# The next pair of heads' bias read in nine pieces over three units, and the first two units without transfers of their tails, in a transformer block on one core

## The chip, the core and the metric

The kernel runs on one core of a Trainium2 chip. The metric is device time in microseconds (us) of one execution. Engines are named as in the profile: PE (TensorE's matmuls), PEld (its weight loads), DVE (VectorE), ACT (ScalarE), POOL (GpSimd) and SP (SyncE), which here does nothing but issue transfers; with "q" behind the name the engine's sequencer is meant.

## The reference, cut to what matters

Three stages follow each other: attention over 4 batches and 8 heads with a position bias, and two feed-forward stages. The change touches attention alone.

```python
B, H, S, D = q.shape                            # 4, 8, 576, 64
scores = (1 / np.sqrt(D)) * q @ k.transpose(0, 1, 3, 2)
x = (log1p(abs(pos_i - pos_j)) / log1p(max(pos_i, 1)))[..., None]
bias = maximum(x @ w1 + b1, 0) @ w2             # 576 x 576 for each of 8 heads
attn = exp(scores + bias - rowmax)
out = (attn / attn.sum(-1)) @ v
x = out as (batch, 576, 512)
x = x + relu(norm(x) @ w_ch1) @ w_ch2
x = x + (gated unit of x) @ w_out
```

## The kernel before, in words

**Stages.** A first stage (0 to about 53 us) computes the bias of all heads and stores it in DRAM (`scr`, `store`, line 358). Attention follows (53 to about 346 us), then the two feed-forward stages (to the end), which the change leaves alone.

**Units.** Attention has 16 units: a pair of heads `hp` (0 to 3) and a batch `b`, with `u = 4 hp + b`. A unit has nine tiles of scores, of 128 rows by 576: four for each head (tiles 0 to 3 and 5 to 8), and tile 4 with the last 64 rows of both. Each tile goes through `S` (scores on PE, line 693), `add` (DVE adds the bias and takes the minimum of the negated sum, line 708), `exp` (ACT, line 723), `T` (PE transposes 512 of the 576 columns, line 728), `hi` (ACT copies the rounded upper part, line 790) and `lo` (DVE subtracts it from the value, line 794). The product with V then takes upper and lower parts as separate terms (`PV`, line 801): for each head h and each half x of the 576 rows there are nine matmuls, of which the ninth multiplies the tails. `Pev`, `O`, `Oev`, `Or`, `fo`, `oc`, `ra`, `rb`, `fx`, `xr` bring the result back into rows, divide it and store it in DRAM (`xs`).

**Tails.** The last 64 of the 576 columns of each tile are transposed apart (`RT`, line 737). The matmul wants their upper parts on one half of the partitions and their lower parts on the other, in the tile `RT`. `RThi` (ACT) writes the upper parts; `RTlo` (DVE, line 763) writes the lower parts to a tile `TL` on the partitions where they arise; `RTd` (line 767) moves them across the partitions by transfers on SP's queue, two for each head (`RTd 0`, `RTd 1`, line 770) and one for tile 4 (`RTd 2`, line 772). The ninth matmul of a head waits for these to land. `RTx` (line 774) is the other way, until now used once at the end: DVE writes the lower parts straight to the other half of the partitions, in two subtractions of 64 partitions in place of one of 128.

**The order of work** is written out by hand: `FIRST` for unit 0, `SEQ` for each of units 1 to 15, `END` for the rest. An entry such as `0 T 3` is a step of the present unit, `-1` of the one before, `1` of the next; each engine runs its own share of the list in that order. `slot` steps (line 894) start transfers: `slot 0` the placing of the next unit's Q (four transfers), `slot 1` the last stores of the unit before, `slot 5` the loads of q and k two units ahead. `vh` (POOL) splits the next v and then issues the load of v two units ahead, `fx` (POOL) divides the result and issues its store. `C` and `cp` are pieces of a conversion of weights that runs beside (DVE, and POOL at `cp`).

**SP's queue.** All of these transfers are issued by SP in the list's order, and each waits for what it needs before the next can be issued.

**Bias.** A pair's bias (nine tiles of 128 x 576) lies in one of two buffers. Before the change `load_bias` (line 265) reads the next pair's whole bias in the unit with b = 2, in eight transfers at slots 1, 4 and 7. The tiles in `TURNED` are stored with their last 64 columns in front, and take two transfers (`turned`, line 260). The first pair's bias is read in the first stage at the places in `READ` (lines 80 and 370), between the last stores of `scr` (`finish`, line 380); two of the last stores are issued by ACT (line 367), the others by SP. Three large stores of `scr` that the first pair doesn't need are held back to unit 0 and the start of unit 1 (`HELD`, line 404).

**Later loads.** In units 12 and 13, weights for the next stage (line 605) are loaded in four transfers; the rows of `xs` (line 627) are loaded behind `fx`, four transfers for each of two batches (line 849).

Of the kernel before, what the change touches and what calls it, by code (L numbers as in the profile page):

```python
# [39 lines left out]
    S 0, S 1, slot 0, slot 1, add 0, add 1, C 0, exp 0, S 2, add 2, T 0, S 5, S 3, hi 0, C 1, add 5, exp 1, lo 0, exp 2, S 6, slot 2, T 1, T 2, add 3,  # L40
    add 6, exp 3, RT 3 0, hi 2, hi 1, lo 2, RT 1 0, S 4, S 7, slot 3, exp 5, lo 1, kh, add 7, T 3, RThi 0, T 5, hi 5, exp 6, hi 3, exp 7, +S 0, RTlo 0,
    lo 5, lo 3, slot 4, slot 5, T 6, RT 6 1, add 4, S 8, RTd 0, exp 4, RT 4 0, vh, RThi 2, T 4, +add 0, +S 2, RTlo 2, hi 4, cp, add 8, lo 4, slot 6,
    hi 6, RTd 2, sq, exp 8, PV 0 0 0 4, slot 7, +S 1, PV 0 0 4 8, lo 6, RT 8 1, T 7, RThi 1, +add 1, +add 2, PV 0 0 8 9, T 8, +S 3, Pev 0 0, RTlo 1,
    hi 7, PV 0 1 0 8, slot 8, lo 7, +exp 0, PV 0 1 8 9, +S 4, +exp 1, hi 8, RTd 1, Pev 0 1
""".split(",")]

LN_AT = [(), (), ((0, 0), (0, 1)), ((0, 2), (0, 3)), ()]
# [3 lines left out]
    O 0 2, RTx 1, lo 8, O 0 3, F 3, PV 1 0 0 5, O 0 0, PV 1 0 5 8, PV 1 0 8 9, Pev 1 0, ra, O 0 1, PV 1 1 0 1, N 0, N 1, Oev 0, fo 0, PV 1 1 1 8,  # L51
    PV 1 1 8 9, O 1 0, Pev 1 1, O 1 2, oc, O 1 1, O 1 3, Or, Oev 1, H 0 0 6, rb, R 0, fo 1, R 1, xr, fx, P 0, H 0 6 12, P 1, P 2, P 3, H 1 0 12
# [27 lines left out]
READ = {20: [2], 27: [0], 29: [1], 32: [3], 35: [4]}  # L80
# [20 lines left out]
def block_kernel(  # L101
# [175 lines left out]

    with ExitStack() as c:
# [306 lines left out]
    def open_first():  # L588
# [11 lines left out]
        for z in range(4):  # L600
# [15 lines left out]
            when(12, 1, ld)  # L616
            when(12, 5 + z, f0)
# [41 lines left out]
    with ExitStack() as c:  # L659
# [176 lines left out]
        def emit_fx(u):  # L836
# [12 lines left out]
            if ("loads", u) in M:  # L849
                M["loads", u]()  # L850
# [38 lines left out]

        def emit_C(u, j):  # L890
# [3 lines left out]
        def emit_slot(u, n):  # L894
# [41 lines left out]
        for u in range(1, NU):  # L936
            for w in SEQ:
# [4 lines left out]
                if 0 <= v < NU:  # L942
# [513 lines left out]
```

## Time and profile before

| what | time |
|---|---|
| three runs | 971.35, 973.46 (median), 974.78 us |
| the profiled execution, its own time | 970.38 us |
| its span, first to last instruction | 968.5 us |
| PE busy over the span | 923.5 us (95%) |
| DVE, ACT, POOL busy | 717.1, 497.5, 416.2 us |
| mean granted clock of TensorE | 0.987 |

The profiled execution is 3.1 us below the median of the runs. In the rows, `out<-in` names what an instruction writes and reads, `x` is a count, and what stands behind `<-` in a list of waits is what ended the wait. A granted clock of 1.00 stands for 2.4 GHz, of 0.50 for 1.2 GHz. Matmuls are pipelined, so that a busy PE isn't PE at its peak.

### The profile page before, as it was taken

To read this page: it belongs to the slowest core of one execution; us is meant where nothing else is said; L and a number is where in the kernel's file an instruction comes from. 1 tells how busy PE (TensorE), PEld (TensorE's weight loads), DVE (VectorE), ACT (ScalarE), POOL (GpSimd) and SP (SyncE) were. 2 spreads that over 40 slices of the span, in tenths; PEclk is the share of its full clock that TensorE was granted. 3 is DMA by queue.
4 is the path that set the end of the run, shared out by engine and by line. 5 is a ranking of instruction groups with operands and counts; after the bars stand their busy time and mean duration, and the time that the engine had idled before them with its cause. 6 is when DMAs were issued, how large, how long until landed. Compare 5 with 4: busy or idle time off the path is not lost.

```text
span 968.5 us, 16023 instructions
## 1 busy us (share of the span) xinstructions
PE 923.5 (95%) x5617; PEld 806.2 (83%) x5617; DVE 717.1 (74%) x1386; ACT 497.5 (51%) x1092; POOL 416.2 (43%) x547
## 2 busy tenths in 40 slices
PE   7878899799899999999999999999999999999998
PEld 2268899799799988888888888888888998988996
DVE  7976799699677978777769897989946556455452
ACT  8967799699788965322223132323222635344340
POOL 0056669668698754321314343333400522234151
PEclk9999899899999999999999999999999999999999
DMA  6877856856866173212022323323230200101001
GB/s 229 268 245 218 240 169 171 248 171 167 251 189 170 40 250 114 66 32 96 23 93 88 120 88 110 100 88 109 92 112 24 116 1 1 44 1 55 1 34 65
DMA packets 65247, 113.77 MB, mean 117 GB/s; under 512 B 13328, under 2 KB 28304, under 8 KB 64912
## 3 DMA queue, kind: packets, MB, share of 16 engines
q1 hardware_dynamic: 64768, 112.18, 37.2%
q8 instruction: 44, 0.72, 0.3%
q10 hardware_dynamic: 400, 0.58, 0.2%
q14 instruction: 35, 0.29, 0.1%
HBM read 70.33 MB, written 28.38 MB: 102 GB/s over the span
## 4 chain that ended last, share of the span: by engine, by line
PE 82%; DMA 7%; DVE 6%; issue 2%; ACT 2%; SPq 0%; POOL 0%; DVEq 0%; ACTq 0%; POOLq 0%
PE psh L124 20%; PE psy L124 20%; PE psa L124 10%; PE psa L1300 6%; PE s L706 6%; PE PB L811 5%; PE psa L1282 5%; PE pt L732 4%; DMA rt<-tl 4%; DVE m L335 2%; DVE ct L712 2%; PE pt L487 1%; DMA scr<-o 1%; PE OB L817 1%; DVE at0l L120 1%
## 5 line engine op out<-in xcount | busy, mean ns | idle before, releaser
L124 PE MATMUL psh<-blk,w1h 128*128 128x512 f32 (+1 forms) x640 | 151.2, 368 | 0.0
L655 ACT ACTIVATE hh<-psh 128x512 fp32r<-128x512 f32 (+1 forms) x80 | 44.1, 553 | 199.2 <-PE psh L124 199.1
L176 POOL TENSOR_TENSOR cvl<-cvl,cvt 128x512 f32<-128x512 f32 x44 | 56.9, 1292 | 205.8 <-DVE cvt L173 182.1
L124 PEld LDWEIGHTS psh<-blk,w1h 128*128 128x128 f32 x640 | 113.4, 189 | 20.5
L712 DVE CUSTOM_DVE_ANT_0 ct<-s,bias 128x576 f32<-128x576 f32 x144 | 106.6, 748 | 16.8 <-ACT rt L117 7.1
L726 ACT ACTIVATE a<-ct,sm 128x576 f32<-128x576 f32 x144 | 111.6, 777 | 4.9 <-DVE sm L712 4.8
L1103 DVE TENSOR_TENSOR x_sb<-psy,x_sb 128x512 f32<-128x512 f32 x144 | 97.3, 683 | 9.1 <-PE psy L124 8.6
L656 DVE SCALAR_TENSOR_TENSOR hl<-psh,hh 128x512 fp32r<-128x512 f32 (+1 forms) x80 | 50.5, 632 | 57.8 <-ACT hh L655 57.8
L124 PE MATMUL psy<-w2h,hh 128*128 128x512 f32 x288 | 90.1, 394 | 0.0
L732 PE MATMUL pt<-ident,a 128*128 128x128 f32 x576 | 87.7, 281 | 1.7 <-DVE at1l L120 1.6
L124 PE MATMUL psy<-w2l,hh 128*128 128x512 f32 x288 | 88.9, 390 | 0.0
L124 PE MATMUL psy<-w2h,hl 128*128 128x512 f32 x288 | 88.7, 389 | 0.0
L124 PE MATMUL psh<-blk,w1l 128*128 128x512 f32 (+1 forms) x320 | 78.7, 368 | 0.0
L706 PE MATMUL s<-kh,q 128*128 128x288 f32 x320 | 74.0, 321 | 1.9 <-DVE sm L712 1.2
L732 PEld LDWEIGHTS pt<-ident,a 128*128 128x128 f32 x576 | 71.3, 145 | 3.8 <-ACT at0h L117 1.5
L706 PE MATMUL s<-kl,q 128*128 128x288 f32 x320 | 67.2, 300 | 0.0
L124 PEld LDWEIGHTS psh<-blk,w1l 128*128 128x128 f32 x320 | 56.9, 189 | 10.0
L124 PEld LDWEIGHTS psy<-w2l,hh 128*128 128x128 f32 x288 | 54.0, 188 | 11.5
L124 PEld LDWEIGHTS psy<-w2h,hl 128*128 128x128 f32 x288 | 54.0, 188 | 11.5
L177 POOL TENSOR_TENSOR cvw<-cvl,cvw 128x512 f32<-128x512 f32 x44 | 59.9, 1362 | 3.4
L124 PEld LDWEIGHTS psy<-w2h,hh 128*128 128x128 f32 x288 | 52.6, 188 | 9.6
L120 DVE TENSOR_TENSOR at1l<-pt,at1h 128x512 fp32r<-128x512 f32 (+1 forms) x80 | 50.3, 630 | 12.6 <-ACT at1h L117 12.6
(185 smaller groups left out, 2136.5 us busy)
## 6 DMA issues: line engine op xcount, KB each, us to landing
r<-in_moe_w_ch_dram SPq DMA_DIRECT2D x32, 512.0 KB, 4.5
k<-in_k_dram SPq DMA_DIRECT2D x16, 640.0 KB, 6.1
q<-q SPq DMA_DIRECT2D x64, 144.0 KB, 2.5
scr<-o SPq DMA_DIRECT2D x24, 295.5 KB, 3.3
v<-in_v_dram SPq DMA_DIRECT2D x16, 320.0 KB, 3.3
q<-in_q_dram SPq DMA_DIRECT2D x16, 288.0 KB, 4.4
bias<-scr SPq DMA_DIRECT2D x8, 576.0 KB, 5.7
bias<-scr SPq DMA_DIRECT2D x8, 512.0 KB, 5.0
```

Of the source, the lines that this page charges most:

```text
L120: (eng or dve).tensor_tensor(out=o, in0=i, in1=hi.bitcast(F32), op=ALU.subtract)
L124: pe.matmul(ps, lhsT=w, rhs=x, start=start and j == 0, stop=stop and j == len(terms) - 1)
L176: pool.tensor_tensor(out=T["l"], in0=T["l"], in1=T["t"].bitcast(F32), op=ALU.mult)
L177: pool.tensor_tensor(out=T["w"], in0=T["l"], in1=T["w"], op=ALU.add)
L656: dve.scalar_tensor_tensor(out=hl[:, f, :n], in0=ps[:, :n], scalar=0.0, in1=hh[:, f, :n].bitcast(F32), op0=ALU.max, op1=ALU.subtract)
L706: pe.matmul(s[:, x, :288], lhsT=w, rhs=m[:, 288 * x:288 * x + 288], start=j == 0, stop=j == len(prs) - 1)
L712: dve.tensor_tensor_reduce(out=ct, in0=s[:, :, :288], in1=bias[UNITS[u][0]][:, n].rearrange("p (a b) -> p a b", a=2), scale=-0.125, scalar ...
L726: act.activation(weights(n), ct.rearrange("p a b -> p (a b)"), AF.Exp, scale=-1.0, bias=mt, accum_out=SU[u % 2][:, n:n + 1])
L732: pe.transpose(PA[k % 2][:, j], e[:, 128 * j:128 * j + 128], ident)
L811: pe.matmul(d, lhsT=w, rhs=m, start=q == 0, stop=q == len(terms) - 1)
L1103: dve.tensor_tensor(out=x_sb[:, t], in0=ps, in1=x_sb[:, t], op=ALU.add)
L1300: pe.matmul(ps[:, z, :288], lhsT=v, rhs=w[:, 288 * z:288 * z + 288], start=(q == 0), stop=(q == len(terms) - 1))
```

## The change

Each pair's next bias is read tile by tile (fourteen transfers in place of eight), at two new steps `B 0` and `B 1` in the units with b = 1, 2 and 3. In units 0 and 1, `RTx` takes the place of `RTlo` and `RTd`; for tile 4 it is one subtraction. The loads of weights in units 12 and 13 are split into two and two; the loads of `xs` rows go from `fx` to `slot 8`, behind the tails' transfers. The last two bias stores are issued by SP in place of ACT, and tiles 3 and 8 of the first pair's bias are read after all stores have been issued. The three lists have new orders: in `SEQ`, `slot 5` now stands behind `RTd 2` and `RTd 0`, `slot 0` and `slot 1` stand earlier. The changed list `FIRST` (with `RTx` for `RTlo` and `RTd`) and the changed list `END` hold otherwise the same steps as before, and are left out below.

```diff
@@ -25,31 +25,32 @@
 TURNED = (0, 2, 5, 7)
 
 SEQ = [w.strip() for w in """
-    -1 ra, 0 add 3, 0 T 0, -1 lo 8, 0 exp 2, 0 exp 3, -1 O 0 1, -1 O 0 0, 0 hi 0, -1 PV 1 0 0 5, 0 add 4, 0 slot 0, 0 slot 1, 0 RT 1 0, 0 T 1, 0 C 0,
-    0 lo 0, 0 RT 3 0, 0 C 1, -1 PV 1 0 5 8, 0 exp 4, -1 O 0 2, 0 hi 1, -1 O 0 3, -1 PV 1 0 8 9, -1 Pev 1 0, 0 S 5, 0 lo 1, 0 S 6, 0 RThi 0, 0 add 5,
-    0 T 2, -1 Oev 0, 0 RTlo 0, 0 hi 2, 0 RT 4 0, 0 slot 2, -1 PV 1 1 0 1, -1 PV 1 1 1 8, 0 slot 3, 0 kh, -1 PV 1 1 8 9, 0 add 6, 0 exp 5, 0 T 3,
-    -1 Pev 1 1, 0 RThi 2, 0 slot 4, 0 S 7, 0 lo 2, -1 rb, 0 hi 3, 0 RTlo 2, -1 O 1 2, -1 O 1 3, -1 O 1 1, 0 exp 6, 0 T 4, 0 slot 5, 0 add 7, 0 lo 3,
-    0 S 8, -1 O 1 0, 1 S 0, -1 fo 0, 0 hi 4, 0 RT 6 1, 0 PV 0 0 0 2, 0 RTd 2, 0 add 8, 0 T 5, 0 exp 7, 0 lo 4, 0 RTd 0, 0 vh, 1 add 0, -1 oc,
-    0 PV 0 0 2 8, -1 Oev 1, 0 T 6, 0 cp, 0 hi 5, -1 fo 1, 1 S 2, 0 PV 0 0 8 9, -1 fx, 0 sq, 0 slot 6, 0 exp 8, 0 lo 5, 0 slot 7, -1 Or, 0 RT 8 1, 0 hi 6,
-    0 lo 6, 0 Pev 0 0, 0 RThi 1, 1 exp 0, 1 S 1, 0 T 7, -1 xr, 0 RTlo 1, 0 T 8, 1 add 1, 0 RTd 1, 0 PV 0 1 0 8, 1 add 2, 0 PV 0 1 8 9, 0 hi 7, 0 slot 8,
-    0 hi 8, 0 lo 7, 1 S 3, 1 exp 1, 1 S 4, 0 Pev 0 1
+    0 T 0, 0 exp 2, 0 slot 0, 0 add 3, 0 exp 3, 0 slot 1, -1 PV 1 0 0 5, 0 C 0, 0 RT 1 0, -1 lo 8, 0 hi 0, 0 S 5, 0 RT 3 0, -1 PV 1 0 5 8, -1 O 0 2,
+    0 add 4, -1 O 0 3, 0 C 1, 0 RThi 0, 0 lo 0, -1 O 0 1, -1 PV 1 0 8 9, 0 T 1, 0 add 5, 0 S 6, 0 B 0, -1 O 0 0, 0 exp 4, -1 Pev 1 0, 0 RTlo 0, 0 RT 4 0,
+    0 hi 1, 0 slot 2, 0 exp 5, -1 ra, 0 slot 3, 0 T 2, 0 lo 1, 0 hi 2, -1 Oev 0, -1 PV 1 1 0 1, 0 add 6, -1 PV 1 1 1 8, -1 PV 1 1 8 9, 0 T 3, 0 lo 2,
+    0 S 7, -1 O 1 0, 0 RThi 2, -1 O 1 2, 0 kh, 0 RTlo 2, -1 Pev 1 1, 0 hi 3, -1 rb, 0 T 4, 0 exp 6, -1 fo 0, -1 oc, 0 hi 4, 0 add 7, 0 lo 3, 0 S 8,
+    -1 O 1 1, 0 RTd 2, 0 slot 4, -1 O 1 3, 0 RTd 0, 0 add 8, 1 S 0, 0 lo 4, -1 Oev 1, 0 slot 5, 0 PV 0 0 0 2, 0 T 5, 0 PV 0 0 2 8, 1 add 0, 0 T 6,
+    0 exp 7, 1 S 2, 0 hi 5, 0 RT 6 1, 0 exp 8, 0 RT 8 1, 0 vh, 0 cp, 0 lo 5, 0 hi 6, 1 S 1, 0 PV 0 0 8 9, -1 fo 1, -1 Or, 0 lo 6, 0 RThi 1, 0 Pev 0 0,
+    -1 fx, 0 RTlo 1, 0 T 7, 0 RTd 1, 0 T 8, 1 add 1, 1 add 2, 0 PV 0 1 0 8, 0 B 1, 0 PV 0 1 8 9, 0 sq, 0 slot 6, 1 exp 0, 0 hi 8, 0 slot 7, 1 S 3,
+    0 hi 7, -1 xr, 1 exp 1, 0 slot 8, 0 lo 7, 0 Pev 0 1, 1 S 4
 """.split(",")]
 
...
+B_AT = [(0,), (1, 2), (3,), (4, 5), (6,), (7, 8)]
...
@@ -77,7 +78,7 @@
     AA AA AA AA AA AA AA AA AD DD AA DA
 """.split()
 
-READ = {20: [2], 27: [0], 29: [1], 32: [3], 35: [4]}
+READ = {20: [2], 27: [0], 29: [1], 35: [3, 8, 4]}
 
 FULL = 24
 GROUPS = ((3, 2), (1, 3))
@@ -262,21 +263,20 @@
         sp.dma_start(out=dst[..., 64:], in_=src[..., :512])
         sp.dma_start(out=dst[..., :64], in_=src[..., 512:])
 
-    def load_bias(hp, z):
+    def load_bias(hp, n):
 
         if hp not in bias:
             new_bias(hp)
-        if z < 2:
-            t = bias[hp][:, 5 * z:5 * z + 4]
-            src = rows(2 * hp, 0, 512)[:, z].rearrange("(n p) j -> p n j", p=128)
-            turned(t[:, ::2], src[:, ::2])
-            sp.dma_start(out=t[:, 1::2], in_=src[:, 1::2])
+        t = bias[hp]
+        if n == 4:
+            for h in range(2):
+                sp.dma_start(out=t[64 * h:64 * h + 64, 4], in_=rows(2 * hp, 512, 64)[:, h])
+            return
+        src = rows(2 * hp, 128 * (n % 5), 128)[:, n // 5]
+        if n in TURNED:
+            turned(t[:, n], src)
         else:
-            for h in range(2):
-                sp.dma_start(out=bias[hp][64 * h:64 * h + 64, 4], in_=rows(2 * hp, 512, 64)[:, h])
-
-
-
+            sp.dma_start(out=t[:, n], in_=src)
 
     with ExitStack() as c:
         p = new_pool("bk", 1, c)
@@ -364,12 +364,11 @@
                 f += heads * PITCH
                 dims, src = [[H * PITCH, 16]], src[heads::H]
             dims += [[16 * (H * PITCH - 1), n], [1, 591]]
-            q = act if heads == 1 and z + n > 34 else sp
-            q.dma_start(out=bass.AP(scr.tensor, scr.offset + f, dims), in_=src.rearrange("p (s j) -> p s j", s=n))
+            sp.dma_start(out=bass.AP(scr.tensor, scr.offset + f, dims), in_=src.rearrange("p (s j) -> p s j", s=n))
 
         def read(k):
-            if k == 4:
-                load_bias(0, 2)
+            if k in (3, 4, 8):
+                load_bias(0, k)
                 return
             t, src = bias[0][:, k::5], rows(0, 128 * k, 128)
             if k % 2:
@@ -613,8 +612,8 @@
                 for k in range(2 if z < 2 else 0):
                     pool.tensor_scalar(out=T["t"][:, k], in0=T["t"][:, k], scalar1=gains[:, 2 * z + k:2 * z + k + 1], scalar2=0.0, op0=ALU.mult, op1=ALU.add)
 
-            when(12, 1, ld)
-            when(12, 5 + z, f0)
+            when(*((12, 1), (12, 1), (12, 8), (12, 8))[z], ld)
+            when(*((12, 5), (12, 6), (13, 1), (13, 2))[z], f0)
             when(13, 4 + z, lambda T=T: pool_copy(T["o"][0], T["t"]))
             when(*LO_AT[z], lambda T=T: split_lo(T["o"][1], T["t"], T["o"][0], pool))
         xT[0] = block_pair(M["wa0"])
@@ -773,6 +772,9 @@
 
         def emit_RTx(u, h):
             p, _ = tails(u, h)
+            if h == 2:
+                split_lo(tail(2, 1, 0), p, tail(2, 1, 1))
+                return
             for x in (1, 0):
                 split_lo(tail(h, x, 1 - x), p[half(x)], tail(h, x, x))
 
@@ -846,8 +848,6 @@
                 M["last x"] = store
             else:
                 store()
-            if ("loads", u) in M:
-                M["loads", u]()
 
         def emit_Or(u):
             pe.transpose(PB[:, 288:416], Pr.rearrange("p h c -> p (h c)"), ident)
@@ -886,6 +886,12 @@
                 split_v(u + 1)
             if u < NU - 2:
                 load_v(u + 2)
+
+        def emit_B(u, j):
+            hp, b = UNITS[u]
+            if hp < 3 and b:
+                for n in B_AT[2 * b - 2 + j]:
+                    load_bias(hp + 1, n)
 
         def emit_C(u, j):
             for f in conv_at.pop((u, j), []):
@@ -911,11 +917,11 @@
                 conv_first(new_pool("arc", 2, M["rc"]))
             if u == 12 and n == 0:
                 open_first()
-            if hp < 3 and b == 2 and n in (1, 4, 7):
-                load_bias(hp + 1, n // 3)
+            if n == 8 and ("loads", u - 1) in M:
+                M["loads", u - 1]()
 
         emit = dict(
-            slot=emit_slot, sq=emit_sq, kh=emit_kh, vh=emit_vh, C=emit_C, cp=lambda u: emit_C(u, 2), S=emit_S, add=emit_add, exp=emit_exp, T=emit_T, hi=emit_hi, lo=emit_lo, RT=emit_RT, RThi=emit_RThi,
+            slot=emit_slot, B=emit_B, sq=emit_sq, kh=emit_kh, vh=emit_vh, C=emit_C, cp=lambda u: emit_C(u, 2), S=emit_S, add=emit_add, exp=emit_exp, T=emit_T, hi=emit_hi, lo=emit_lo, RT=emit_RT, RThi=emit_RThi,
             RTlo=emit_RTlo, RTd=emit_RTd, RTx=emit_RTx, PV=emit_PV, Pev=emit_Pev, O=emit_O, Oev=emit_Oev, fo=emit_fo, fx=emit_fx, Or=emit_Or, oc=emit_oc, ra=emit_ra, rb=emit_rb, xr=emit_xr,
         )
         def first_T(j):
@@ -939,7 +945,9 @@
                 v, args = u + int(du), list(map(int, args))
                 if v == NU - 1 and name in ("RTlo", "RTd") and args == [1]:
                     continue
-                if 0 <= v < NU:
+                if v == 1:
+                    name = {"RTlo": "RTx", "RTd": ""}.get(name, name)
+                if 0 <= v < NU and name:
                     emit[name](v, *args)
                 elif v == NU and name in ("S", "add") and args[0] < 4 - (name == "add"):
                     (first_T if name == "S" else first_split)(*args)
```

## Rows read from the trace of the kernel before

**Rows 1.** The page, part 1: busy time, share of the span, count.

```profile
PE 923.5 (95%) x5617; PEld 806.2 (83%) x5617; DVE 717.1 (74%) x1386; ACT 497.5 (51%) x1092; POOL 416.2 (43%) x547
```

**Rows 2.** PE's waits, 45 to 350 us: total, times, longest.

```profile
PE PB L811 <- DMA rt<-tl: 24.1, 6, 6.0
PE pt L732 <- DVE at1l L120: 1.6, 2, 1.3
```

**Rows 3.** Windows by unit: length; PE, PEld, DVE, ACT, POOL busy; clock; DMA; GB/s.

```profile
53.34:68.97 15.63, 11.18 (x73) 9.53 (x72) 10.35 (x25) 9.83 (x24) 10.53 (x10) 0.94 0.76 239
68.97:91.61 22.64, 17.84 (x126) 17.62 (x125) 13.48 (x35) 15.38 (x40) 10.08 (x11) 0.89 0.80 241
91.61:107.45 15.84, 15.84 (x130) 15.68 (x129) 15.16 (x37) 15.54 (x42) 12.39 (x15) 1.00 0.76 218
107.45:129.59 22.14, 17.76 (x127) 17.51 (x126) 14.20 (x37) 15.52 (x39) 12.31 (x15) 0.85 0.69 212
...
176.76:200.88 24.12, 18.09 (x127) 17.81 (x126) 14.24 (x36) 15.89 (x40) 13.55 (x16) 0.86 0.66 201
...
247.96:269.69 21.73, 17.18 (x127) 16.94 (x125) 14.22 (x37) 15.53 (x39) 13.24 (x16) 0.92 0.65 200
...
285.21:303.17 17.96, 15.75 (x128) 15.55 (x127) 13.38 (x35) 15.10 (x40) 14.69 (x20) 1.00 0.60 169
303.17:321.10 17.93, 15.78 (x128) 15.55 (x127) 13.29 (x35) 15.10 (x40) 14.01 (x18) 1.00 0.50 144
321.10:336.75 15.65, 15.34 (x124) 14.94 (x123) 15.35 (x41) 14.96 (x40) 12.85 (x28) 1.00 0.14 35
```

**Rows 4.** SP's timeline in unit 6: start, time to issue, line, transfer.

```profile
169.36 0.58 SPq L262 DMA_DIRECT2D bias<-scr  x1
...
173.67 0.42 SPq L216 DMA_DIRECT2D k<-in_k_dram  x1
...
175.28 2.17 SPq L770 DMA_DIRECT2D rt<-tl  x2
```

**Rows 5.** The chain of waits, 170 to 190 us: start, length, what.

```profile
175.28 9.01 DMA rt<-tl
```

**Rows 6.** SP's timeline at the end of unit 4, without bias.

```profile
148.67 0.38 SPq L843 DMA_DIRECT2D xs<-x  x1
149.14 1.11 SPq L770 DMA_DIRECT2D rt<-tl  x2
```

**Rows 7.** The tails' transfers (line 770), from issue to landing.

```profile
DMA to landing us min/median/max: 1.9/2.0/9.1
```

**Rows 8.** PE's timeline, the matmul that waits for the transfers of rows 6.

```profile
153.79 0.38 PE L811 MATMUL PB<-rt,v 128*128 128x288 f32 x1
```

**Rows 9.** SP's timeline, the later loads in units 12 and 14.

```profile
278.81 2.00 SPq L605 DMA_DIRECT2D t<-wc  x4
...
308.07 1.75 SPq L627 DMA_DIRECT2D t<-xs  x4
```

**Rows 10.** Window 67 to 83 us, with the columns of rows 3.

```profile
67.00:83.00 16.00, 11.21 (x63) 10.92 (x64) 7.62 (x18) 8.07 (x21) 6.79 (x7) 0.79 0.99 287
```

**Rows 11.** SP's timeline in unit 0, the held stores of the bias.

```profile
62.51 1.21 SPq L368 DMA_DIRECT2D scr<-o  x2
```

**Rows 12.** DVE's groups by form to 350 us: busy us, mean ns, idle before.

```profile
L120 DVE TENSOR_TENSOR tl<-s,rt 128x256 fp32r<-128x256 f32 x31 | 13.0, 420 | 3.6 <-PE s L706 1.6 <-ACT rt L117 0.5 <-DMA bias<-scr 0.2
L120 DVE TENSOR_TENSOR rt<-s,rt 64x256 fp32r<-64x256 f32 x2 | 0.8, 422 | 0.1
```

**Rows 13.** SP's waits, 45 to 350 us.

```profile
SPq L843 <- POOL x L840: 23.1, 13, 4.2
```

**Rows 14.** DMA issues: what, count, KB each, median us to landing.

```profile
bias<-scr SPq DMA_DIRECT2D x8, 512.0 KB, 5.0
bias<-scr SPq DMA_DIRECT2D x8, 64.0 KB, 4.6
```

**Rows 15.** The page, part 5: the group of `exp` on ACT.

```profile
L726 ACT ACTIVATE a<-ct,sm 128x576 f32<-128x576 f32 x144 | 111.6, 777 | 4.9 <-DVE sm L712 4.8
```

More of the change, by code (lines that the diff above doesn't have):

```diff
@@ L39 @@
 FIRST = [w.strip() for w in """
[L40 to L44, printed above, removed]
+    S 0, add 0, exp 0, S 1, S 2, add 1, exp 1, add 2, S 5, T 0, hi 0, S 3, exp 2, T 1, add 5, RT 1 0, slot 0, lo 0, exp 5, S 6, T 2, hi 2, add 3, hi 1,
+    add 6, S 4, slot 1, lo 2, C 0, exp 3, lo 1, S 7, T 3, T 5, C 1, add 4, slot 2, add 7, exp 6, slot 3, hi 3, hi 5, S 8, kh, slot 4, RT 3 0, lo 3,
+    exp 4, add 8, slot 5, +S 0, RThi 0, vh, T 4, lo 5, +S 1, T 6, exp 8, +add 0, RT 4 0, hi 4, RTx 0, PV 0 0 0 4, RThi 2, RTx 2, lo 4, exp 7, hi 6, +S 2,
+    lo 6, RT 8 1, cp, slot 6, RT 6 1, PV 0 0 4 8, RThi 1, +add 1, PV 0 0 8 9, sq, T 8, Pev 0 0, T 7, PV 0 1 0 8, +S 3, +add 2, RTx 1, +exp 0, hi 7,
+    PV 0 1 8 9, hi 8, slot 7, +S 4, lo 7, +exp 1, slot 8, Pev 0 1
 """.split(",")]
+B_AT = [(0,), (1, 2), (3,), (4, 5), (6,), (7, 8)]
 LN_AT = [(), (), ((0, 0), (0, 1)), ((0, 2), (0, 3)), ()]
@@ L50 @@
 END = [w.strip() for w in """
-    O 0 2, RTx 1, lo 8, O 0 3, F 3, PV 1 0 0 5, O 0 0, PV 1 0 5 8, PV 1 0 8 9, Pev 1 0, ra, O 0 1, PV 1 1 0 1, N 0, N 1, Oev 0, fo 0, PV 1 1 1 8,
-    PV 1 1 8 9, O 1 0, Pev 1 1, O 1 2, oc, O 1 1, O 1 3, Or, Oev 1, H 0 0 6, rb, R 0, fo 1, R 1, xr, fx, P 0, H 0 6 12, P 1, P 2, P 3, H 1 0 12
+    RTx 1, O 0 0, PV 1 0 0 5, lo 8, F 3, O 0 2, PV 1 0 5 8, O 0 1, O 0 3, N 0, PV 1 0 8 9, PV 1 1 0 1, Pev 1 0, Oev 0, PV 1 1 1 8, PV 1 1 8 9, N 1,
+    O 1 0, ra, Pev 1 1, rb, oc, H 0 0 6, Or, O 1 3, R 0, O 1 2, R 1, xr, O 1 1, Oev 1, fo 1, fo 0, fx, P 0, H 0 6 12, P 1, P 2, P 3, H 1 0 12
 """.split(",")]
```

## The prediction, made before the changed kernel was run

> **What bounds the kernel now.** I read the busy times first, then PE's waits, then the units' windows, then SP's queue around the long ones. PE is busy for 95% of the span [rows 1], so only PE's waits and its clock can be won back. In attention, PE's waits are nearly all of one kind: six waits of the tails' matmul for the tails' transfers, 24.1 us in all, the longest 6.0; the next kind has 1.6 us [rows 2].
>
> The windows run from the first `add` of a unit to that of the next [rows 3]. Nine of the sixteen are alike: those of units 2, 4, 5, 6, 8, 9, 10, 12 and 15 last 15.49 to 15.84 us, 15.70 in the mean (the first and the last of them stand in the rows), and PE is busy through them. Six are longer: units 1 (22.64), 3 (22.14), 7 (24.12), 11 (21.73), 13 (17.96) and 14 (17.93). Over 15.70 that is 6.94 + 6.44 + 8.42 + 6.03 + 2.26 + 2.23 = **32.3 us**. It is more than the 24.1 us of waits, because the granted clock is 0.85 to 0.92 in the four longest: after a long wait a stretch at the lower level (0.50) follows.
>
> SP's queue says why. In unit 6 it issues most of the next pair's bias from 169.36 us on, then q and k, and only then the tails' transfers, at 175.28 [rows 4]; those land 9.01 us later [rows 5], where the median is 2.0 [rows 7]. Transfers of this queue land about in the order of issue. Units 2 and 10, the other two with b = 2, do the same to units 3 and 11; in unit 0 the held stores, 2.4 MB, stand in front [rows 11]; in units 12 and 14 it is four loads, with the tails' transfers behind them [rows 9].
>
> **The change part by part.** The sum is made against the profiled execution's 970.4 us.
>
> *Bias in nine pieces.* A pair's bias is 2.65 MB (nine times 128 x 576 x 4 bytes); at the 287 GB/s of a full queue [rows 10] that is 9.2 us in one unit, and becomes 3.1 us in each of three. `B 0` (one tile, 1.0 us) stands ahead of `RTd 2`, behind the last stores of the unit before; `B 1` (two tiles, 2.1 us) stands behind `RTd 1`. What is queued behind `B 1` is the placing of the next Q, which its first matmul wants some 7.5 us of PE work later: nothing. There are six more issues for each pair, 18 in all, by 0.58 us [rows 4] 10.4 us of SP, which isn't always issuing: it waits 23.1 us for POOL's results alone [rows 13]. Nothing; without that cover at most 0.58 x 5 = 2.9 us in a unit.
>
> *`slot 5` behind `RTd 2` and `RTd 0`.* The loads of q and k (0.95 MB, 3.3 us) no longer delay these two, but now stand closer to `RTd 1`, together with v (0.33 MB) and the store of x (0.26 MB): 1.54 MB, 5.4 us from about 4.5 us before `RTd 1`, so it lands up to 1 us later. The slack: in unit 4 `RTd 1` is issued by 150.25 [rows 6], lands some 2.0 us later by the median [rows 7], at about 152.2, and its matmul runs at 153.79 [rows 8], so 1.6 us are over. Nothing, but tight.
>
> *Units 0 and 1 without tails' transfers.* The tail wait of unit 1's window goes. Added: for each head two subtractions of 0.422 us in place of one of 0.420 [rows 12], so 0.85 us of DVE for two heads, tile 4 as before. DVE is busy for 10.35 of 15.63 and 13.48 of 22.64 us there [rows 3]; with unit 1 at 15.7 it still has 1.4 us over after the addition. Nothing; without cover 1.7 us.
>
> *Later loads.* They move behind the tails' transfers or are halved; their 2.26 + 2.23 us stand in the 32.3.
>
> *Last stores from SP, tiles 3 and 8 read later.* Two issues by 0.6 us [rows 11] leave ACT and join SP. The first pair's tiles 3 and 8 may come up to 1.2 us later, or earlier, because the read no longer holds SP ahead of the last stores. I take 0, between -1 and +1.2.
>
> *What is late next: the queue itself.* Units 0 and 1 moved 15.63 x 239 + 22.64 x 241 = 9.2 MB [rows 3]. Without the wait they have 31.3 us for it, and unit 1 gets 0.9 MB of the next bias more, the tails' 0.3 MB less: 9.8 MB at 287 GB/s [rows 10] are 34.1 us, so a backlog of 2.8 us goes into unit 2. Unit 2 moved 218 x 15.84 = 3.5 MB of the 4.5 that the queue can, will have a third of the bias in place of most of it, and works the backlog off; but its first tails may wait. Between 0 and 5 us (2.8 and as much again of slow clock); I take 1.5.
>
> *New orders.* The matmuls are the same. In the regular windows PE has no idle time to lose, ACT is busy for 15.54 of 15.84 us and DVE for 15.16 [rows 3], so another order can only leave PE alone or make it wait. From below 0; from above 0.5 us a unit, as much as ACT has free, 7.5 in all. Nearest is unit 2's window, where two such full engines cost PE nothing; I take 0.1 a unit, 1.5. `END` has PE as full: 0, give or take 0.5.
>
> Here a rule speaks against the change. By the rows a 64 KB column part takes no longer to land (4.6 us) than the 512 KB part issued just ahead of it (5.0) [rows 14], so it holds the queue hardly at all. The Trainium skill ("DMA: Bandwidth & Descriptors", section "Rules for kernel authors") says that many small transfers should be joined into a large one, and that under 64 KB one pays mostly overhead; the column parts of the new single tiles have 32 KB. By that rule the sum would be worse; by the rows it stays.
>
> **Sum**: 970.4 - 32.3 + 1.5 + 1.5 = 941.1 us. The median of the runs lies 3.1 us above the profiled execution, which gives **944 us** for a median.
>
> **The rivals.**
>
> *The queue stays full to unit 3.* The backlog above isn't worked off: unit 2's tails wait like before, and the 6.44 us of unit 3's window stay: 944 + 6.4 = 950, with unit 1 late as well up to 956. For it: a DMA share of 0.99 [rows 10]. Against: the load two units ahead leaves slack. 15%.
>
> *Small pieces hold the queue.* Each 32 KB part costs the time of a whole small transfer, 2.0 us [rows 7]. Where the queue is full, in units 1 and 2, there are three (tiles 0, 2 and 5): 944 + 6 = 950. Against: rows 14. 3%. This is what the skill's rule named above would do here.
>
> *The orders don't keep PE fed.* 0.5 to 1 us a unit for DVE or ACT: 944 + 6 to + 13.5 = 950 to 958. For it: ACT's and DVE's busy shares. Against: the old order, as full, has no such wait. 12%.
>
> *The spreading doesn't do what it says*, and in the units with bias the tails still wait, half of 6.44 + 8.42 + 6.03: 944 + 10.4 = 954. 3%.
>
> *Slower than before:* `RTd 1` hangs on POOL. SP issues the store of x just ahead of it [rows 6] and waits for POOL's division there, 23.1 us in 13 units [rows 13]. In the new list `vh` stands behind `oc`, and `Oev 0`, which POOL's `fo 0` needs, behind one more `exp` on ACT (0.78 us [rows 15]). If POOL ends later by more than the slack of 1.6 us, PE waits in each of 13 units. At 4.1 us late that is 13 x 2.5 = 32.5 us and all is lost; with the slow clock, 980. For it: POOL is busy for 12 to 14.7 of 15.7 us. Against: the shift that I can read is that one `exp`, and a rounded copy at most; under the slack. 5%.
>
> **How the numbers follow.** The forecast, all waits gone and 0 to 6 us of small new ones, has 62%: 937 (nothing new, and the first unit a little shorter) to 950. With the queue's case and the small pieces (18%) up to 956 the range holds 80%; the orders' case lies half inside. So 937 to 956. A measurement of this kernel can tell about 0.3% (2.9 us) from no change. All but the last rival are faster by more: 0.93; 0.02 for something between; 0.05 slower.
>
> **What would show it.** Right: PE's waits for `rt<-tl` gone or under 5 us in all; windows of units 3, 7, 11, 13 and 14 at 15.5 to 16; tails' landings at 2 to 3 us; a granted clock of 1.00 from unit 2 on; no `rt<-tl` transfers before unit 2. The queue's rival: unit 2's or 3's window over 18 us. The orders' rival: all windows over 16.2, PE waiting for DVE or ACT. The slower one: PE waiting for `rt<-tl` in many units, and SP's wait at line 843 or its like longer than 23 us. The forecast is wrong if the sum of the windows hasn't fallen by about 30 us, or if a new wait stands outside attention.

## The result, and the profile after

| | median of runs | profiled execution | its span |
|---|---|---|---|
| before | 972.4 us (970.93 to 974.78) | 970.38 us | 968.5 us |
| changed | 933.85 us (932.2 to 936.71) | 936.71 us | 934.9 us |

The ratio is 0.960, with a 95% interval of 0.957 to 0.964. The change is faster, as forecast, but by 38.6 us, more than the range allowed: 933.85 lies 3 us below its lower end of 937, and 10 us below the forecast of 944.

The page of the changed kernel, part 1, to set beside [rows 1]:

```profile
PE 914.6 (98%) x5617; PEld 798.7 (85%) x5617; DVE 716.4 (77%) x1390; ACT 494.7 (53%) x1092; POOL 419.0 (45%) x547
```

PE's busy time fell by 8.9 us although its instructions are the same 5617: a matmul that runs at the lower clock counts as busy for longer (before, the tails' matmul takes 0.295 us in the median, and 0.58 at 184.42 us, where the granted clock is 0.50). PE's waits in the changed kernel, 45 to 320 us, answer to [rows 2]:

```profile
PE s L705 <- DMA q<-q: 2.1, 1, 2.1
...
PE PB L813 <- DMA rt<-tl: 0.3, 1, 0.3
```

The 24.1 us of waits for the tails are gone but for 0.3. The longest wait is a new one, for the transfers that place Q. The windows from unit to unit answer to [rows 3] and have the same columns:

```profile
53.43:64.19 10.76, 9.75 (x69) 8.48 (x69) 9.57 (x24) 9.02 (x22) 10.34 (x10) 1.00 0.83 256
64.19:80.42 16.23, 16.21 (x130) 15.70 (x129) 15.31 (x39) 15.70 (x44) 8.63 (x11) 1.00 0.87 273
80.42:96.67 16.25, 15.81 (x129) 15.46 (x127) 15.69 (x38) 15.24 (x40) 14.11 (x17) 1.00 0.78 253
96.67:112.19 15.52, 15.52 (x128) 15.40 (x126) 14.37 (x36) 15.09 (x41) 13.04 (x16) 1.00 0.86 253
...
158.79:174.32 15.53, 15.53 (x128) 15.53 (x127) 14.39 (x36) 15.33 (x42) 14.96 (x18) 1.00 0.74 220
...
221.10:236.63 15.53, 15.53 (x128) 15.53 (x127) 14.40 (x36) 15.01 (x41) 13.20 (x16) 1.00 0.78 218
...
252.17:268.22 16.05, 15.79 (x128) 15.55 (x127) 13.54 (x35) 15.35 (x40) 14.09 (x21) 1.00 0.67 197
268.22:285.54 17.32, 15.18 (x122) 14.96 (x121) 13.56 (x34) 15.20 (x41) 14.58 (x19) 0.99 0.74 207
```

These are units 0 to 3, 7, 11, 13 and 14. Units 3, 7 and 11 have lost 6.62, 8.59 and 6.20 us and last as long as PE is busy, at a granted clock of 1.00. Unit 1 has lost 6.41. What the sum had not counted is the first line: unit 0 lasts 10.76 us in place of 15.63, 4.87 less. Unit 14 is still long.

SP's timeline in unit 6 (143 to 159 us) shows the new order of the queue, to set beside [rows 4]:

```profile
143.10 0.40 SPq L217 DMA_DIRECT2D k<-in_k_dram  x1
...
146.37 1.11 SPq L769 DMA_DIRECT2D rt<-tl  x2
147.53 0.58 SPq L279 DMA_DIRECT2D bias<-scr  x1
...
154.32 0.43 SPq L279 DMA_DIRECT2D bias<-scr  x1
155.96 0.64 SPq L771 DMA_DIRECT2D rt<-tl  x1
156.69 1.19 SPq L769 DMA_DIRECT2D rt<-tl  x2
157.94 0.58 SPq L211 DMA_DIRECT2D q<-in_q_dram  x1
```

The bias now stands behind `RTd 1` (146.37) and, as one tile, ahead of `RTd 2` (155.96); q and k come last. The transfers of line 769, `RTd 0` and `RTd 1`, land like this, from issue (minimum, median, longest), to set beside [rows 7]:

```profile
DMA to landing us min/median/max: 1.9/2.2/6.0
```

The longest is not at 2 to 3 us, as the prediction's signs had it, but PE hardly waits for it.

The new wait stands in unit 14. SP's timeline there, and then PE's:

```profile
275.58 1.76 SPq L626 DMA_DIRECT2D t<-xs  x4
277.43 2.40 SPq L237 DMA_DIRECT2D q<-q  x4
```

```profile
284.62 0.51 PE L705 MATMUL s<-kh,q 128*128 128x288 f32 x2 [2.14 <-DMA q<-q]
```

The later loads of `xs` (1 MB) stand ahead of the placing of the next Q, and the first scores of unit 15 wait for that Q. What they no longer cost the tails, they cost Q, in part.

**Where the time went**, by the windows of the two profiled executions: unit 0 -4.87, unit 1 -6.41, units 3, 7 and 11 -21.4, units 13 and 14 -2.5, the other units together -0.4, the end of attention with unit 15 +1.5, all else +0.5. That is -33.6, and the spans differ by 33.6. The 1.5 us at the end come with a slow clock behind the new wait:

```profile
285.54:312.66 27.12, 26.39 (x199) 25.14 (x198) 23.21 (x53) 22.21 (x55) 18.34 (x37) 0.94 0.25 71
```

In another execution of the same kernel (`again`, below), whose wait was 1.7 us in place of 2.1, the same stretch took 25.65 us at a clock of 1.00; before it took 25.59. The medians differ by 38.6, because the changed kernel's profiled execution was the slowest of its four, and that of before faster than all of its four.

### The profile page after: what moved, and what is told of

Same layout as the page of the kernel before. It is cut to its first block, busy times and chain, and to the rows that moved or that the text cites. A ratio compares the mean times of both kernels' runs of the same rounds, so it can differ in the third digit from the quotient of the medians.

```text
span 934.9 us, 15977 instructions
## 1 busy us (share of the span) xinstructions
PE 914.6 (98%) x5617; PEld 798.7 (85%) x5617; DVE 716.4 (77%) x1390; ACT 494.7 (53%) x1092; POOL 419.0 (45%) x547
## 4 chain that ended last, share of the span: by engine, by line
PE 86%; DVE 6%; DMA 3%; POOL 2%; ACT 2%; issue 1%; SPq 0%; POOLq 0%; DVEq 0%; ACTq 0%
PE psh L125 21%; PE psy L125 21%; PE psa L125 11%; PE s L705 6%; PE psa L1308 6%; PE PB L813 6%; PE psa L1290 5%; PE pt L731 5%; DVE m L335 4%; PE pt L486 1%; PE OB L819 1%; DMA q<-q 1%; DMA rt<-tl 1%; PE s L741 1%; PE pt L347 1%
## 5 line engine op out<-in xcount | busy, mean ns | idle before, releaser
L731 PE MATMUL pt<-ident,a 128*128 128x128 f32 x576 | 84.4, 274 | 0.4 <-DVE at0l L121 0.4
L731 PEld LDWEIGHTS pt<-ident,a 128*128 128x128 f32 x576 | 68.6, 142 | 1.1 <-DVE at0l L121 0.7
```

The source lines that it names most:

```text
L731: pe.transpose(PA[k % 2][:, j], e[:, 128 * j:128 * j + 128], ident)
```

## The experiments

The theory after reading the two traces: each long wait was a small transfer behind large ones on SP's queue; where the small one was moved ahead, or isn't needed, the wait is gone; the first unit is shorter because of its new order. The rivals stand with each run. Times are medians. Where the next pair's bias is concerned, "units with bias" are the nine with b = 1, 2, 3 and hp < 3.

### The first unit: the order, or the tails

`first_old` has the old list `FIRST`, only with `RTx` for `RTlo` and `RTd`:

```diff
-    S 0, add 0, exp 0, S 1, S 2, add 1, exp 1, add 2, S 5, T 0, hi 0, ...
+    S 0, S 1, slot 0, slot 1, add 0, add 1, C 0, exp 0, S 2, add 2, T 0, ...
```

> The changed kernel with the old order in unit 0; its tails still go without transfers. Theory 'order': unit 0's window, which fell from 15.6 to 10.8 us, is back at 15 to 16, and the kernel takes 938 to 940. Rival 'tails' (the first unit is shorter because its tails need no transfers): the window stays at 10.8 to 12, 934 to 935.

Measured: 940.04 us, ratio 0.966 (0.963 to 0.970), 6.2 us more than the changed kernel. Its first unit's window:

```profile
53.56:69.43 15.87, 11.16 (x73) 9.47 (x73) 10.96 (x27) 9.83 (x24) 10.55 (x10) 0.94 0.88 280
```

15.87 us, with PE, DVE and ACT each busy for 9.8 to 11.2 of them, as before [rows 3]. The tails are direct here and the unit isn't shorter: it is the order. What it removes are waits of PE for DVE and ACT within the unit. The longest kinds before (53.34 to 68.97 us), and then the only one after (53.43 to 64.19 us):

```profile
PE pt L732 <- DVE at1l L120: 1.3, 1, 1.3
PE s L742 <- ACT a L726: 1.2, 1, 1.2
PE s L706 <- DVE sm L712: 1.2, 3, 0.4
```

```profile
PE s L705 <- DVE sm L711: 0.9, 2, 0.6
```

`tails_back` keeps the new lists but moves the tails of units 0 and 1 by transfers again:

```diff
-                if v == 1:
-                    name = {"RTlo": "RTx", "RTd": ""}.get(name, name)
-                if 0 <= v < NU and name:
+                if 0 <= v < NU:
```

and, in `FIRST`, `RTlo` and `RTd` for each `RTx`.

> The changed kernel with the tails of units 0 and 1 moved by transfers again, right behind their subtraction. Theory 'queue' (these transfers stand behind the held stores): a wait of 4 to 6 us for rt<-tl in unit 0 or 1 and a stretch of slow clock, 939 to 943; unit 0's window stays near 10.8. Rival 'order' (the new order alone would have freed them): no wait over 1 us, 934 to 935.

Measured: 944.64 us, ratio 0.971 (0.968 to 0.974), 10.8 more than the changed kernel. PE's waits, then the windows of units 0 and 1:

```profile
PE PB L809 <- DMA rt<-tl: 8.6, 2, 8.4
```

```profile
53.80:64.44 10.64, 9.49 (x68) 8.35 (x68) 9.48 (x23) 8.97 (x22) 10.22 (x10) 1.00 0.82 259
64.44:90.97 26.53, 18.17 (x130) 17.55 (x129) 13.87 (x37) 15.85 (x43) 10.36 (x12) 0.81 0.71 219
```

The matmul that waits in unit 1, before and in `tails_back`:

```profile
77.31 0.58 PE L811 MATMUL PB<-rt,v 128*128 128x288 f32 x1 [4.79 <-DMA rt<-tl]
```

```profile
75.87 0.58 PE L809 MATMUL PB<-rt,v 128*128 128x288 f32 x1 [8.36 <-DMA rt<-tl]
```

The theory of the queue holds and the price was set too low. The short first unit stays short, but PE comes to a transfer that lands only 1.4 us earlier than before, and waits 8.4 us instead of 4.8. Units 0 and 1 together take 37.17 us in place of 38.27: the order of unit 0 and the direct tails pay together, and the 5 us of the first are worth little without the second.

`stores_act` undoes the last part of the first stage: two of the last stores on ACT again, tiles 3 and 8 read at place 32.

```diff
-READ = {20: [2], 27: [0], 29: [1], 35: [3, 8, 4]}
+READ = {20: [2], 27: [0], 29: [1], 32: [3], 35: [4]}
+            q = act if heads == 1 and z + n > 34 else sp
```

> The changed kernel with the last two bias stores issued by ACT and tiles 3 and 8 read at place 32, as before. Theory 'order': unit 0's window stays near 10.8 us, time 933 to 936. Rival 'stores' (the first unit is shorter because its last tiles of bias come sooner): the window is 13 us or more, 936 to 939.

Measured: 935.69 us, ratio 0.963 (0.960 to 0.966), 1.8 more, which isn't clear of the noise: its runs go from 935.32 to 938.44 us, fourteen runs of the changed kernel from 932.1 to 937.05. The first unit's window, and then DVE's wait for the bias in it (50 to 66 us), here and in the changed kernel:

```profile
53.06:65.27 12.21, 9.75 (x69) 8.47 (x69) 9.56 (x23) 9.13 (x22) 10.59 (x10) 1.00 0.68 198
```

```profile
DVE ct L712 <- DMA bias<-scr: 1.4, 1, 1.4
```

```profile
DVE ct L711 <- DMA bias<-scr: 0.6, 1, 0.6
```

The window is between the two theories: 1.45 us longer than in the changed kernel, of which 0.8 is DVE's longer wait for the bias and 0.37 an earlier start. In other profiled executions with the changed first unit it lasts 10.43 to 11.47 us. So about 1 us of the first unit's 4.9 may hang on the earlier tiles; the order is the larger part.

### The spreading, and what it needs

`spread_only` is the kernel before, old orders, with nothing but the bias in nine pieces:

```diff
-            if hp < 3 and b == 2 and n in (1, 4, 7):
-                load_bias(hp + 1, n // 3)
+    0 slot 1, 0 B 0, 0 RT 1 0,   ...   0 RTd 1, 0 B 1, 0 PV 0 1 0 8,
```

> The kernel before, with its old orders, and only the bias read in nine pieces over three units. Theory 'spreading': units 3, 7 and 11 lose 6.4, 8.4 and 6.0 us and are near 15.7, the other long windows (1, 13, 14) stay: 972.4 - 20.9 = 951.5, between 949 and 954. Rival 'order' (q and k still stand ahead of RTd 2 and RTd 0, so with bias they hold the tails up): half of it or less, 961 or more.

Measured: 971.74 us, ratio 0.998 (0.995 to 1.001): no gain that can be measured. Theory 'spreading' is wrong and the rival's bound of 961 or more holds. PE's waits, 45 to 350 us, and the windows of units 3 and 4:

```profile
PE PB L811 <- DMA rt<-tl: 21.6, 9, 4.2
```

```profile
108.49:125.10 16.61, 15.77 (x129) 15.54 (x127) 15.03 (x36) 15.14 (x40) 12.28 (x15) 1.00 0.70 197
125.10:145.33 20.23, 17.20 (x127) 16.95 (x126) 13.99 (x37) 15.93 (x40) 13.21 (x16) 0.92 0.66 190
```

Unit 3 is mended but for 0.8 us, and unit 4, which was regular, now waits. Six waits have become nine: those of units 1, 13 and 14 stay, and the three in units 3, 7 and 11 (15.0 us) are now six in units 3, 4, 7, 9, 11 and 12 (11.6 us). Spreading the bias mostly spreads the wait.

`no_spread` is the other half: the changed kernel, all pieces in one unit again (`B 0` and `B 1` are left empty).

```diff
+            if hp < 3 and b == 2 and n in (1, 4, 7):
+                for k in ((0, 2, 1, 3), (5, 7, 6, 8), (4,))[n // 3]:
+                    load_bias(hp + 1, k)
```

> The changed kernel, with the same nine pieces all read in the unit with b = 2, at slots 1, 4 and 7. Theory 'spreading': units 2 or 3, 6 or 7 and 10 or 11 wait for the tails again, 6 to 8 us each with the slow clock: 933.9 + 18 to 21 = 952 to 955. Rival 'order' (the tails' transfers now stand ahead of the loads of q and k, which is enough): under 6 us in all, 934 to 940.

Measured: 951.76 us, ratio 0.978 (0.976 to 0.981), 17.9 more. PE's waits, and the windows of units 3, 7 and 11:

```profile
PE PB L813 <- DMA rt<-tl: 12.4, 4, 4.8
```

```profile
96.54:116.29 19.75, 16.06 (x128) 15.59 (x127) 14.35 (x37) 15.47 (x40) 13.30 (x17) 1.00 0.82 229
162.88:184.05 21.17, 17.33 (x128) 17.11 (x128) 14.51 (x37) 15.71 (x42) 15.22 (x18) 0.92 0.70 211
230.65:252.62 21.97, 17.14 (x128) 16.91 (x127) 14.43 (x37) 15.28 (x41) 13.26 (x16) 0.92 0.67 198
```

The waits of before are back at their old places, somewhat shorter: the three windows are 16.3 us over 15.53 in all, where before they were 20.9 over 15.70. The order alone doesn't free them either.

Which part of the order does the spreading need? q and k, 0.95 MB, stand ahead of `RTd 2` in the old list. Two runs move this one step, `slot 5`. `slot5_ahead` puts it back in the changed kernel; `spread_slot5` takes `spread_only` and moves it behind `RTd 0`:

```diff
-    -1 O 1 1, 0 RTd 2, 0 slot 4, -1 O 1 3, 0 RTd 0, 0 add 8, 1 S 0, 0 lo 4, -1 Oev 1, 0 slot 5,
+    -1 O 1 1, 0 slot 5, 0 RTd 2, 0 slot 4, -1 O 1 3, 0 RTd 0, 0 add 8, 1 S 0, 0 lo 4, -1 Oev 1,
```

```diff
-    ... 0 T 4, 0 slot 5, 0 add 7, ... 0 RTd 0, 0 vh,
+    ... 0 T 4, 0 add 7, ... 0 RTd 0, 0 slot 5, 0 vh,
```

> The changed kernel with one step moved: slot 5 (the loads of q and k two units ahead) stands just ahead of RTd 2 again. Theory 'q and k' (spreading alone gained nothing because these 0.95 MB, made late by the bias, stand ahead of the tails): waits of 1 to 3 us for rt<-tl in most of the nine units with bias, with stretches of slow clock, 945 to 960. Rival 'whole order' (the place of slot 5 is one of many): waits in three units at most, 934 to 940.

> The kernel before with the bias spread, and slot 5 moved behind RTd 0, all other orders old. Theory 'q and k': units 3, 7 and 11 lose their waits without new ones in the other units with bias, 950 to 956. Rival 'whole order': as with spreading alone, 962 to 973.

Measured: `slot5_ahead` 948.03 us, ratio 0.977 (0.973 to 0.981), 14.2 more than the changed kernel. PE's waits, 45 to 350 us:

```profile
PE PB L813 <- DMA rt<-tl: 11.6, 6, 3.7
```

The longest of the six stands in unit 13, which has no bias to read:

```profile
261.13:283.10 21.97, 18.25 (x128) 17.97 (x127) 13.50 (x35) 15.35 (x41) 14.13 (x21) 0.84 0.65 184
```

It is 5.9 us longer than in the changed kernel, behind loads of weights with q and k. So a part of the 14.2 us is the cost of this step for the later loads and not for the bias. The other five waits (7.9 us) are in the windows of units 4, 6, 7, 8 and 11; the theory had looked for them in most of the nine units.

`spread_slot5` 954.19 us, ratio 0.983 (0.980 to 0.985), 17.5 less than with spreading alone. PE's waits, and the windows of units 3, 7, 11 and 14:

```profile
PE PB L811 <- DMA rt<-tl: 10.9, 3, 6.3
```

```profile
108.23:123.75 15.52, 15.52 (x128) 15.52 (x127) 14.90 (x36) 15.16 (x40) 12.84 (x15) 1.00 0.84 251
170.41:186.34 15.93, 15.93 (x129) 15.69 (x128) 15.24 (x36) 15.61 (x42) 14.43 (x17) 1.00 0.78 228
233.15:248.49 15.34, 15.34 (x127) 15.34 (x126) 14.72 (x36) 15.02 (x39) 13.78 (x16) 1.00 0.76 220
280.13:304.69 24.56, 18.23 (x128) 17.88 (x127) 13.60 (x34) 15.32 (x40) 14.47 (x20) 0.86 0.49 144
```

Shown from both sides: one step's place decides whether the spreading pays. With it, the units with bias have no wait left but that of unit 1 (4.2 us), which stands behind the held stores. The last line shows the other side of it: the loads of `xs` behind `fx`, which cost unit 14 2.2 us before, now cost 8.9.

`seq_old` has the whole old order of units 1 to 15 and all else new.

> The changed kernel with the old order of units 1 to 15 (the steps of the bias put in), all else new. Theory 'q and k': the waits of the spread-only kernel in units 2 to 11 and one of 2 us or more in unit 12 or 13, without the one in unit 1 and with the short first unit: 950 to 960. Rival 'first' (the order of unit 0 and the direct tails carry the gain): 934 to 943.

Measured: 954.49 us, ratio 0.983 (0.980 to 0.987), as the theory had it; eight waits for the tails:

```profile
PE PB L813 <- DMA rt<-tl: 15.3, 8, 2.9
```

Against `slot5_ahead` the rest of the new order of these units is worth 6.5 us.

### The later loads

`loads_old` puts the loads of weights and of `xs` back:

```diff
-            if n == 8 and ("loads", u - 1) in M:
-                M["loads", u - 1]()
+            if ("loads", u) in M:
+                M["loads", u]()
-            when(*((12, 1), (12, 1), (12, 8), (12, 8))[z], ld)
+            when(12, 1, ld)
```

(the first two added lines stand at the end of `fx`).

> The changed kernel with the later loads where they were: four weight loads at once in unit 12, rows of xs behind fx. Theory 'structure' (the loads only moved from ahead of the tails to ahead of Q): a wait for rt<-tl of some 2.2 us comes back in units 13 and 14, the wait for q in unit 14 goes: 933 to 936.5. Rival 'gain' (the later loads are worth the 4.5 us that the prediction counted): 938 to 939.

Measured: 942.92 us, ratio 0.969 (0.966 to 0.972), 9.1 more; both theories set it too low. Unit 14's window and PE's wait:

```profile
270.30:293.53 23.23, 18.41 (x128) 18.03 (x127) 13.72 (x34) 15.50 (x40) 15.11 (x19) 0.85 0.52 155
```

```profile
PE PB L813 <- DMA rt<-tl: 6.1, 3, 4.8
```

In the new order the same loads at the old place hold the tails for 4.8 us in place of 2.15, and the clock falls behind it (0.85). `spread_slot5`, with the old order but for one step, has a wait of 6.3 us there. What the two share is the new place of `slot 5`, with q, k and v just ahead of the store of x. At the old place SP first waits for that store to land, 2.4 us before, 3.4 in `loads_old` and 5.1 in `spread_slot5`, and `RTd 1` stands behind this wait. That it is the whole cause wasn't tested.

`again` and `again_5` are the changed kernel itself. `loads_behind_q` and `loads_behind_q_5` are one kernel, in which the loads of the first batch come behind the placing of Q:

```diff
-            if n == 8 and ("loads", u - 1) in M:
-                M["loads", u - 1]()
+            if n == 1 and u == 14:
+                M["loads", 12]()
+            if n == 8 and u == 15:
+                M["loads", 14]()
```

> The changed kernel once more, to have it beside the variants on one chip and to know how its one long wait behaves from execution to execution. Both theories: 933.9 us, ratio to before 0.957 to 0.964. Theory 'structure' (the placing of Q stands behind 1 MB of loads in every execution): the wait of some 2.1 us for q in unit 14 is there again. Rival 'hiccup' (one late transfer in one execution): it is gone, and unit 14's window is 15.5.

> The first batch's loads of rows of xs are issued in slot 1 of unit 14, behind the placing of the next Q, in place of slot 8 of unit 13. Theory 'structure': the wait for q (2.1 us and the slower clock behind it, 3.9 us by the windows of units 14 and 15) goes, time 930 to 932. Rival 'hiccup': the median stays at 933.9 within 1 us.

> The changed kernel once more, beside the next one, for a median of more runs: 933.8 within 1 us, with the wait for q in unit 14.

> The kernel with the loads behind the placing of Q once more. Theory 'the wait counts': it took 934.2 before only because other stretches of its runs were slow by chance (its runs' mean clocks were 0.995 to 0.998); beside the changed kernel on the same chip it is faster by 1.5 to 2 us, 932. Rival 'given back': the wait of 1.7 to 2.1 us is gone in the profile, but the same time is lost elsewhere: no difference over 0.7 us.

Measured: 933.71 and 934.47 us for the changed kernel, 934.2 and 933.81 for the other; ratios 0.960 and 0.961 against 0.960 and 0.960, each give or take 0.003 or 0.004. PE's wait in `again`, and unit 14's window in `again` and in `loads_behind_q`:

```profile
PE s L705 <- DMA q<-q: 1.7, 1, 1.7
```

```profile
267.23:283.98 16.75, 15.06 (x122) 14.85 (x121) 13.56 (x35) 15.20 (x41) 14.87 (x19) 1.00 0.74 211
```

```profile
267.90:283.43 15.53, 15.53 (x128) 15.53 (x127) 13.45 (x35) 15.02 (x41) 14.54 (x19) 1.00 0.77 231
```

The long window is one of structure and can be removed: with the loads behind Q it is as short as all others. Its wait isn't always put down to Q. In the third trace of the changed kernel (`again_5`) the expectation failed: unit 14 lasts 16.46 us, and the same scores wait 1.4 us there for DVE and not for Q. In the median nothing comes of the variant that two tries could show, though the slowest of its twelve runs took 934.9 us, where the changed kernel's slowest of fourteen took 937.05. The window is 0.9 to 1.8 us shorter and the mean of all runs 0.5 us lower (933.8 against 934.3), which is within the noise; a gain of 1 us isn't excluded. The variant doesn't beat the changed kernel by a measurable amount.

### Small pieces

`halves` cuts every transfer of the next pairs' bias in two by rows: 26 for a pair in place of 14, the same bytes (the two transfers of tile 4 are left whole).

```diff
+        for r in ((slice(0, 64), slice(64, 128)) if hp else (slice(0, 128),)):
+            if n in TURNED:
+                turned(t[r, n], src[r])
+            else:
+                sp.dma_start(out=t[r, n], in_=src[r])
```

> The changed kernel with each of the next pairs' bias transfers cut in two by rows, 28 for a pair in place of 14, the same bytes. Theory 'bytes' (the queue is held by bytes): 933 to 936, no wait for rt<-tl over 1 us. Rival 'small pieces' (each transfer holds the queue for a time of its own, 2 us): 4 to 5 more in each of nine units, 8 to 10 us more queue time in each, waits of several us in most of them, 950 or more.

Measured: 943.13 us, ratio 0.971 (0.968 to 0.974), 9.3 more, between the two theories. PE's waits:

```profile
PE PB L814 <- DMA rt<-tl: 6.7, 8, 1.9
```

Twelve more transfers for each of three pairs, 36 in all, cost 0.26 us each in the mean. So a transfer has a price beside its bytes, but not 2 us. It is a rough figure: 1.5 us of the waits stand in unit 13, which reads no bias, and the halves also span 64 partitions in place of 128. The traces point to SP's time to issue: ahead of `RTd 2` (line 771, here 772) SP waits for DVE 11 times, 20.4 us in all, in the changed kernel, but only 2 times, 3.6 us, in `halves`, so SP itself now mostly comes late. But the median time to landing of `RTd 0` and `RTd 1` also grows, from 2.2 to 2.8 us, and no run separates SP's time from the queue's.

## Why the prediction was wrong, point by point

**Right:** what bounds the kernel (waits of PE for the tails behind large transfers, and the clock behind them), and that all six waits for the tails go: the windows of units 1, 3, 7 and 11 came out within 0.6 us of the 15.7 forecast, the granted clock is 1.00 from the first unit to the new wait, and the slower rival (`RTd 1` behind POOL), that of the orders and that of the queue (units 2 and 3 took 16.25 and 15.52 us, not over 18) didn't come true.

**The size** was wrong. In the profiled execution the sum said 941.1 and 936.7 was measured. By the windows:

- *The step that failed: "another order can only leave PE alone or make it wait."* It was argued from the regular windows, where PE is always busy. Unit 0's row stood among the same rows, with PE busy for 11.18 of 15.63 us, DVE for 10.35 and ACT for 9.83: no engine was full there, and an order could win. It won 4.87 us; PE's idle time there was waits for DVE and ACT, which the new order has all but removed. `first_old` gives 6.2 us for it in the median. The prediction named this only as "a little shorter".
- *The allowances.* 1.5 us for a backlog of the queue and 1.5 for the orders were added. Units 1 and 2 took 0.53 and 0.55 over 15.70; the ten units 3 to 12 took 15.53 for the most part, 1.5 less in all than ten times 15.70. So 3.0 were added where on balance 0.4 were won.
- *Later loads: "stand in the 32.3".* Of 4.5 us, unit 14's 2.2 were mostly not won in this execution (17.32 us after 17.93): the list of what is queued behind the moved loads was drawn up for the tails, and not for Q, which `slot 0` places right behind them. Unit 14 and the end are 3.2 us longer than forecast. This error goes the other way.
- *From the profile to the median.* 3.1 us were added because the profiled execution of before lay below its median by that much. It isn't a property of the kernel: that of the changed kernel lay 2.9 us above. This alone makes 6 of the 10 us between 944 and 933.85.

**The reasons**, tested one by one, were less right than the sum. *"Nothing, but tight"* for `slot 5`: it is the step without which the spreading gains nothing that can be measured (971.7 against 954.2), and undoing it costs 14.2 us, unit 13's share included. The list of what stood ahead of the tails in unit 6 was also not complete: 0.5 MB of a later stage's weights (line 567) were issued there too, at 171.00 us, which the change leaves. The prediction gave all of the gain of units 3, 7 and 11 to the nine pieces; the pieces alone would have been the rival "doesn't do what it says", and gained less than its half. *Direct tails in units 0 and 1*: 6.94 us were forecast, undoing them costs 10.8, because the wait ends when the queue has landed its backlog (77.3 us before, 75.9 in `tails_back`) and PE comes 5 us earlier. *Small pieces*: the Trainium skill ("DMA: Bandwidth & Descriptors", "Rules for kernel authors") advises to join small transfers, and the sum went against it by the landing times of [rows 14]. In the change the pieces cost nothing that the windows show; cut once more, into parts of 16 to 144 KB, they cost 9.3 us, so the advice has a price here, 0.26 us for each transfer in the mean.

Undone one at a time, the order of unit 0, direct tails, spreading, later loads and the first stage's stores cost 6.2 + 10.8 + 17.9 + 9.1 + 1.8 = 45.8 us, more than the 38.6 that all of them win: they share waits, and none has a price of its own. The last of the five isn't clear of the noise. The new order of units 1 to 15 (20.6 us when undone as a whole) isn't in this sum, and the new `END` was not undone by itself; the end's 25.65 us in `again`, where the clock didn't fall, against 25.59 before shows no gain or loss from it.

## What to carry to other kernels

Where a small transfer waits on a queue, list everything ahead of it at the moment of its issue: spreading one large transfer helps only if the other large ones move behind the small one too. A gain up front is real only if the next fixed time (here the landing of a queue's backlog) moves with it, so parts have to be priced together. Look for room to win in the rows where no engine is full, and don't carry the offset of one profiled execution to a median.

## What the runs showed that was not expected

Spreading 2.65 MB from one unit over three, with nothing else changed, left the time where it was (0.998) and turned six waits of 24.1 us in all into nine of 21.6. And a wait's price depends on what stands around it: the same four loads at the same place cost unit 14 2.2 us before and 7.7 in the changed order (23.23 against 15.53), 4.8 of it as the wait, and the rest in a window whose mean clock is 0.85.
